# Cosine attention and a hard-swish feed-forward: shared items for the first pairs, transposing DMAs from item 8, a listed order of units, and a halved last unit

## The chip, the cores and the metric

The kernel runs on one core of one Trainium2 chip. The metric is the device time of one execution in microseconds (us). The median of three runs before the change is 427.83 us, the lowest 425.83 and the highest 430.05.

## The reference

```python
q_n = q / (norm(q) + 1e-6); k_n = k / (norm(k) + 1e-6)      # [8, 12, 448, 64], fp32
attn = softmax(q_n @ k_n.T / 0.1)                           # rows of 448
x = (attn @ v).transpose(0, 2, 1, 3).reshape(3584, 768)
h = x @ w_in                                                # 768 -> 2048
out = (h * clip(h + 3, 0, 6) / 6) @ w_out                   # 2048 -> 768, fp32
```

There are 8 batches of 12 heads, 448 rows a head and 64 columns a row. After the attention all heads of a row stand side by side and pass through two matrix products with a hard swish between them.

## The kernel before, in words

**Pairs and items.** The work on the attention goes by pairs of heads: pair i holds two heads of batch i // 6, so there are 48 pairs. The inputs come in by items: from item 2 on, item j holds q or k of two neighbouring pairs, 64 partitions for each of them and seven rows of a head in one partition (128 x 896 fp32, 448 KB). Items 2d and 2d+1 are q and k of pairs 2d and 2d+1; from `XJ` on the order is k first. Only items 0 and 1 are different: item 0 is pair 0 alone, q in the lower 64 partitions and k in the upper, and item 1 is pair 1 in the same way. They come by four DMAs each, half of them from ScalarE's queue.

**Steps.** The whole order of the first 18 pairs is written out by hand in `PLAN` (L19), a list of tokens that `run` (L659) takes one by one. Each engine gets its instructions in this order and waits, in order, for what they need. The tokens are:

- `LQ.j` loads item j (`load_qk`, L165), `LV.d` loads v of pairs 2d and 2d+1 (`load_v`, L186), both on SyncE's (SP's) queue. `W` starts the next of eight loads of the weights (L607), four of `w_in` and then four of `w_out`, from GpSimd (POOL), which cast to bf16.
- `SQ.j.e.c.n` squares n of the columns of item j from column c, on the engine e: v is VectorE (DVE), p is POOL, a is ScalarE (ACT). `RE.j` sums the squares (DVE), `NO.d` makes 1/norm of items 2d and 2d+1 from them with four small ACT instructions, and `NM.j.e` normalises item j into bf16.
- Then an item is transposed, in one of two ways. `TR.j` (L293) does it with seven matmuls into a PSUM bank, and `CQ.i` and `CK.i` copy q and k of pair i out of it. `XD.j` (`crossbar`, L304) does it with one transposing DMA on SP's queue, straight into a tile `tT` in SBUF; the scores read q from there, and only k is copied, by `CK.i` (L345). `CS.i` makes the last key block: by copies, or, after an XD, by two small POOL copies into `km` for two pairs at once. Even items of the second kind share one `tT` buffer, so the next even XD must wait for the `CK` and `CS` of the two pairs before it. Which way an item takes is set by `XJ`, which is 14 here (L105).
- `SC.i.g` are the scores of pair i in four groups, `EX.i.g` their exponentials on ACT, `VA.i.g` their products with v (PE). `VC.i` casts v to bf16 ahead of that. `FI.i` divides by the sums (DVE).
- The result is turned back into `xT`, again in one of two ways: `BK.i` with four matmuls and then `CX.i`, a copy from PSUM; or `XB.i` (`back_crossbar`, L492) with one transposing DMA on SP's queue.
- `U` issues the next unit of the feed-forward part on PE. There are two kinds: `mm1_unit` (L506), six matmuls of 448 columns that make one block of h for one batch (it needs `xT` of all six pairs of the batch; 16 per batch), and `mm2_unit` (L539), 16 matmuls of 384 columns that make a tile of the output (it needs all 16 blocks of h, and all weights loaded). `UA` and `UV` are what follows a unit: ACT's relu or copy, and DVE's product or copy with the store.
- `DP.n` and `D.n` are n matmuls on zeros, whose result nobody reads. `OPEN` changes over from PSUM tiles of two banks for the scores to a ring of six single banks.

**Which unit comes next** is set by `units` (L584), a rule for how many first and second products go with each pair; `stream` (L687) is the list made from it. The first 36 of them are issued by `PLAN`, and the rest by a loop over pairs 18 to 47 (L697), with three or four units a pair. After the last pair come the remaining units; the last `mm2_unit` has `end=True`: its output tile is copied in two halves of 64 partitions, the upper by ACT and the lower by DVE, and the second of its two stores goes from ACT's queue.

**SP's queue** runs in order as well: a DMA that waits for its input holds up all DMAs behind it. Eight semaphores are used in turn for it, so that at most eight DMAs are under way.

Of the kernel before, what the change touches and what calls it, by code (L numbers as in the profile page):

```python
# [60 lines left out]
def kernel(  # L61
# [43 lines left out]
    XJ = 14  # L105
# [59 lines left out]
    def load_qk(j, e="s"):  # L165
        needs(("NM", j - NR))
        raw_of[j] = raws[j % NR]
        if j < 2:
            for g in range(2):
                for i, x in enumerate((q, k)):  # L170
                    f = x[0, j + HP * g].rearrange("(p c) d -> p (c d)", c=7)
                    r = raw_of[j][64 * i : 64 * i + 64, g, :, :].rearrange("p c d -> p (c d)")
                    engines[e[i % len(e)]].dma_start(out=r, in_=f)
            return
# [6 lines left out]
    def load_v(d, e="s"):  # L186
        needs(("VC", 2 * (d - NV)), ("VC", 2 * (d - NV) + 1))
        b, n = 2 * d // HP, 2 * d % HP
        for g in range(2):
            f = v[b, HP * g + n : HP * g + n + 2].rearrange("i (p c) d -> p i (c d)", c=7)  # L190
            t = vr[d % NV][:, 2 * g : 2 * g + 2, :, :].rearrange("p i c d -> p i (c d)")
            for half in range(2):
                o = t[64 * half : 64 * half + 64, :, (1 - half) * D : (5 - half) * D]
                engines[e].dma_start(out=o, in_=f[:, :, 3 * half * D : (3 * half + 4) * D])
# [127 lines left out]
    def source(i, keys_of):  # L322
        j, x = (i, keys_of) if i < 2 else (i // 2 * 2 + (keys_of ^ (i >= XJ)), i % 2)
# [7 lines left out]
    def copy_q(i, e="v"):  # L331
        needs(("SM", i - 4))
        z, x, key = source(i, 0)
        if i >= 2:
            copy(e, qT[i % 4][:, 0:S], z[:, :, x, :])
            return
        q2 = qT[i % 4][:, 0:S].rearrange("p (c e) -> p c e", e=64)
        for h, n in ((0, 4), (1, 3)):
            o, f = q2[:, 4 * h : 4 * h + n, :], z[:, h : h + 2 * n - 1 : 2, x, :]
            if e == "a":  # L340
                nc.scalar.copy(out=o, in_=f)
            else:
                nc.vector.tensor_copy(out=o, in_=f)
# [195 lines left out]
    def mm2_unit(b, t, m, end=False):  # L539
        assert not weights  # L540
        g = gT[(b // 2) % 2]
        ps, key = bank_of(None, 1)
        for fc in range(FCN):
# [9 lines left out]
        cols = slice(m * MH, (m + 1) * MH)  # L553

        def store():
            o = sb.tile([128, MH], FP32, name="o", tag="o", bufs=4)
            if end:
                nc.scalar.copy(out=o[64:128, :], in_=ps[64:128, 0:MH])
                nc.vector.tensor_copy(out=o[0:64, :], in_=ps[0:64, 0:MH])
            elif on_act:  # L560
                nc.scalar.copy(out=o[:, :], in_=ps[:, 0:MH])  # L561
            else:
                nc.vector.tensor_copy(out=o[:, :], in_=ps[:, 0:MH])  # L563
            unread[key] = 0
            for e in range(2):
# [4 lines left out]
                eng = nc.scalar if end and e else nc.sync  # L570
                eng.dma_start(out=r[:, cols], in_=o[64 * e : 64 * e + 64, :])
# [208 lines left out]
```

## Time and profile before

| what | value |
|---|---|
| three runs, median | 427.83 us |
| the profiled execution, its own time | 426.68 us |
| its span, from the first to the last instruction | 424.7 us |
| PE, DVE, ACT, POOL busy in the span | 410.5, 220.1, 271.4, 184.0 us |
| DMA: moved, mean rate | 65.04 MB, 153 GB/s |
| XD (`tT<-nrm`): count, median from issue to landing | 34, 3.2 us |
| XB (`xT<-on`): count, median from issue to landing | 36, 3.5 us |
| loads of q and k, of v, of weights: median to landing | 4.3 to 4.6, 4.1, 9.0 to 9.6 us |
| clock granted to PE, mean | 0.997 |

The span is the part that the profile shows; 1.98 us of this execution's time lie outside of it. Busy time is an average over parts of the kernel with different limits, so the stretches of the span have to be read one by one. Matmuls are pipelined, and PE counts as busy in many of the short gaps between them: to see how well it is used, the work in a stretch has to be summed from the units.

### The profile page before, as it was taken

The numbers are of one execution on the slowest core, as the hardware profiler recorded it, in microseconds if no ns is written. First come the engines' busy times: TensorE is split into PE (matmuls) and PEld (weight loads), VectorE is DVE, ScalarE is ACT, GpSimd is POOL, SyncE is SP. The second block draws the span as 40 slices with busy tenths as digits, with TensorE's granted clock in tenths as the row PEclk, the third lists the DMA queues.
The fourth block names the chain that finished last, engine by engine and source line by source line (L and its number), as shares of the span: only waits on it lengthen the run. The fifth ranks groups of instructions, "written<-read, shape, count | busy, mean of one in ns | idle before, by whom it ended". The sixth has DMA issues, their size and how long they took to land.

```text
span 424.7 us, 9220 instructions
## 1 busy us (share of the span) xinstructions
PE 410.5 (97%) x3561; PEld 241.0 (57%) x3561; DVE 220.1 (52%) x427; ACT 271.4 (64%) x593; POOL 184.0 (43%) x188
## 2 busy tenths in 40 slices
PE   5899899999999999999999999999999999999995
PEld 2666456455655556555555555555555555655563
DVE  6896888856335554565455454555554343315411
ACT  4999799868547765766766775676765775105400
POOL 6997488515504555364464464374462200000000
PEclk9999999999999999999999999999999999999998
DMA  7999799998849769666978767667666241230033
GB/s 231 310 192 294 142 285 184 203 212 206 183 103 195 183 168 149 165 172 150 178 190 136 177 154 160 163 167 170 164 158 96 68 69 32 69 75 20 0 76 75
DMA packets 90828, 65.04 MB, mean 153 GB/s; under 512 B 55456, under 2 KB 89248, under 8 KB 90784
## 3 DMA queue, kind: packets, MB, share of 16 engines
q1 hardware_dynamic: 86672, 57.60, 59.1%
q0 software_dynamic: 3712, 6.29, 8.4%
q10 hardware_dynamic: 400, 0.56, 0.5%
q8 instruction: 28, 0.46, 0.5%
q14 instruction: 16, 0.13, 0.1%
HBM read 47.19 MB, written 11.01 MB: 137 GB/s over the span
## 4 chain that ended last, share of the span: by engine, by line
PE 80%; DMA 4%; DVE 2%; ACT 2%; POOL 1%; SPq 1%; issue 1%; POOLq 0%; DVEq 0%; ACTq 0%
PE M L546 22%; PE M L512 19%; PE PV L449 9%; PE Y L546 6%; PE Z L546 6%; PE Z L512 5%; PE M L410 5%; PE Y L512 5%; DMA tT<-nrm 3%; DMA vr<-in_v_dram 2%; PE Y L410 1%; PE Z L410 1%; DVE n L222 1%; ACT at L428 1%; DVE gT L527 1%
## 5 line engine op out<-in xcount | busy, mean ns | idle before, releaser
L546 PEld LDWEIGHTS <-gT 128*128 128x128 bf16 x896 | 87.4, 98 | 59.3 <-issue 0.2
L428 ACT ACTIVATE at<-M 128x448 bf16<-128x448 f32 x203 | 98.2, 564 | 28.0 <-PE M L410 17.9
L512 PEld LDWEIGHTS <-w_in_sb 128*128 128x128 bf16 x768 | 74.0, 98 | 66.8 <-issue 2.9
L512 PE MATMUL M<-xT,w_in_sb 128*128 128x448 bf16 x498 | 102.3, 353 | 0.2 <-DVE gT L527 0.2
L546 PE MATMUL M<-w_out_sb,gT 128*128 128x384 bf16 x576 | 97.9, 326 | 0.0
L253 POOL TENSOR_TENSOR nrm<-raw,r 128x896 bf16<-128x896 f32 (+1 forms) x48 | 79.7, 1666 | 37.6 <-ACT r L241 32.3
L527 DVE SCALAR_TENSOR_TENSOR gT<-u,M 128x448 bf16<-128x448 bf16 x83 | 51.3, 619 | 47.0 <-ACT u L521 45.5
L210 POOL TENSOR_TENSOR sq<-raw 128x896 f32<-128x896 f32 (+5 forms) x43 | 65.8, 1535 | 15.7 <-DVE n L222 8.4
L449 PEld LDWEIGHTS <-at 128*128 128x128 bf16 x1344 | 53.7, 98 | 24.0 <-issue 16.8
L521 ACT ACTIVATE u<-M,half_bias 128x448 bf16<-128x448 f32 x83 | 54.0, 651 | 19.9 <-PE M L512 18.2
L449 PE MATMUL PV<-vx,at 128*128 128x65 bf16 (+1 forms) x1344 | 64.4, 198 | 0.1
L222 DVE TENSOR_REDUCE n<-sq 128x14 f32<-128x896 f32 (+1 forms) x50 | 51.7, 1040 | 2.6 <-POOL sq L210 2.1
L367 POOL COPY km<-tT 64x128 bf16<-64x128 bf16 x34 | 9.8, 289 | 96.5 <-DMA tT<-nrm 34.4
L410 PE MATMUL M<-tT,kz 64*128 64x448 bf16 (+1 forms) x181 | 33.3, 353 | 2.2 <-DMA tT<-nrm 0.9
L428 ACT ACTIVATE at<-Z 128x448 bf16<-128x448 f32 x47 | 26.6, 566 | 11.8 <-PE M L410 11.8
L465 DVE TENSOR_TENSOR on<-PV,rc 128x512 bf16<-128x512 f32 x48 | 33.2, 691 | 1.9 <-DVE rc L464 0.2
L561 ACT COPY o<-M 128x384 f32<-128x384 f32 x19 | 9.1, 478 | 39.0 <-PE M L546 35.2
L546 PE MATMUL Y<-w_out_sb,gT 128*128 128x384 bf16 x176 | 30.4, 326 | 0.0
L563 DVE COPY o<-M 128x384 f32<-128x384 f32 x16 | 8.9, 558 | 41.3 <-PE M L546 41.3
L512 PE MATMUL Z<-xT,w_in_sb 128*128 128x448 bf16 x138 | 29.9, 353 | 0.0
L428 ACT ACTIVATE at<-Y 128x448 bf16<-128x448 f32 x44 | 25.1, 570 | 5.6 <-PE Z L410 5.3
L512 PE MATMUL Y<-xT,w_in_sb 128*128 128x448 bf16 x132 | 28.6, 353 | 0.0
(82 smaller groups left out, 333.5 us busy)
## 6 DMA issues: line engine op xcount, KB each, us to landing
vr<-in_v_dram SPq DMA_DIRECT2D x96, 128.0 KB, 4.1
out_dram<-o SPq DMA_DIRECT2D x111, 96.0 KB, 2.2
raw<-in_k_dram SPq DMA_DIRECT2D x23, 448.0 KB, 4.6
raw<-in_q_dram SPq DMA_DIRECT2D x23, 448.0 KB, 4.3
w_in_sb<-in_moe_w_in_dram POOLq DMA_DIRECT2D x4, 768.0 KB, 9.6
w_out_sb<-in_moe_w_out_dram POOLq DMA_DIRECT2D x4, 768.0 KB, 9.0
xT<-on SPq DMA_TRANSPOSE x36, 3.5
tT<-nrm SPq DMA_TRANSPOSE x34, 3.2
```

The lines of the kernel that those rows point to most:

```text
L210: engines[e].tensor_tensor(out=o, in0=i, in1=i, op=ALU.mult)
L222: nc.vector.tensor_reduce(out=n2s[d % 2][:, j % 2, c], in_=sq[:, :, :, :].rearrange("p g c d -> p (g c) d")[:, c, :], axis=AX.X, op=ALU.add,)
L253: engines[e].tensor_tensor(out=nrm[:, :, g, :].rearrange("p c g d -> p g c d"), in0=raw_of[j][:, g, :, :], in1=rs[d % 2][3][:, j % 2, :] . ...
L367: nc.gpsimd.tensor_copy(out=km[p, :, p], in_=z[p, 3, :, :])
L410: nc.tensor.matmul(o, ks, qt[rows], start=True, stop=True)
L428: nc.scalar.activation(out=o, in_=x, func=AF.Exp, scale=inv_tau)
L449: nc.tensor.matmul(o, at[:, n, q_cols(i // HP, j)], mv, start=(name == "A0" and j % 2 == 0), stop=last, skip_group_check=True,)
L465: nc.vector.tensor_tensor(out=on[:, :, :, :].rearrange("p (b j) h d -> p b (j h) d", b=2), in0=pv4[:, :, :, 0:D], in1=rc[:, :, :].to_broad ...
L512: nc.tensor.matmul(ps[:, 0:S], w_in_sb[:, cc, fc * 128 : (fc + 1) * 128], x[:, cc, 0:S], start=(cc == 0), stop=(cc == CC - 1),)
L521: nc.scalar.activation(out=u[:, :], in_=ps[:, 0:S], func=AF.Relu, bias=half_bias[:, :], scale=1.0 / 6.0)
L527: nc.vector.scalar_tensor_tensor(out=g[:, fc, c0 : c0 + S], in0=u[:, :], scalar=1.0, in1=ps[:, 0:S], op0=ALU.min, op1=ALU.mult,)
L546: nc.tensor.matmul(ps[:, 0:MH], lhs, w_out_sb[:, fc, m * MH : (m + 1) * MH], start=(fc == 0), stop=(fc == FCN - 1),)
```

## The change

Five things change.

1. Items 0 and 1 become like the others: item 0 is q of pairs 0 and 1, item 1 is k of them. `LQ.0` is one DMA, `LQ.1.1` and `LQ.1.0` are two, one for each head of the pairs, all on SP's queue. Their copies `CQ` and `CK` are then as for other items.
2. `XJ` goes from 14 to 8: items 8 to 13 are transposed by DMA instead of PE. In the list, pairs 6 to 11 are also turned back by `XB` instead of `BK` and `CX`.
3. The first 80 units are taken in the order of kinds that a string `ORDER` lists. Both orders issue 30 first and 6 second products in the list; in the new one all second products come after 29 first ones, in the old one the first comes after 23.
4. `PLAN` has another order throughout, with other engines for some squares, copies and casts. The last weight loads come later in it, and it has 82 matmuls of `DP` in 31 places instead of 55 in 12.
5. The last unit of all is split into two of 192 columns. Each half is copied by one engine and stored; the second store of the last half goes from ACT's queue.

```diff
-PLAN = [
-    "LQ.0.sa D.10 LQ.1.sa SQ.0.v.0.4 SQ.0.v.4.3 SQ.0.a.7.5 SQ.0.p.12.1 SQ.1.a.4.1 SQ.0.p.13.1 LQ.3 RE.0.0",
...
-    "SC.7.1 SC.7.2 TR.9 VA.6.3 EX.7.1 W EX.7.2 CS.8.a SQ.10.a.0.7 SC.7.3 CK.8.a U U VC.7.v CS.9.v U FI.6 CK.9.v",
-    "RE.11 EX.7.3 UA SQ.13.a.0.3 RE.10 UA UV BK.6 U VA.7.0 UA UA SQ.13.p.3.4 UV VA.7.1 SC.8.0 U NO.5 NM.10.p UV UA",
...
+ORDER = "11111111111111111111111111111222212211221112111211221112111121121111122111211121"
+PLAN = [
+    "LQ.0 LQ.1.1 SQ.0.v.6.2 SQ.0.a.0.6 LQ.1.0 LQ.3 SQ.1.a.7.4 SQ.0.v.8.6 SQ.1.a.11.3 DP.5 RE.0.0 RE.0.1 SQ.1.p.4.3",
+    "RE.1.1 SQ.1.a.0.4 DP.2 RE.1.0 NO.0.0 SQ.3.a.0.7 DP.3 NM.0.v.1 NM.0.v.0 NO.0.1 RE.3 LQ.2 NM.1.p.1 DP.2 D.10",
+    "TR.0.Y DP.7 LQ.5 SQ.2.a.0.7 NM.1.p.0 RE.2 DP.2 SQ.5.p.0.7 TR.1.Z DP.2 NO.1 LQ.6 LQ.4 CK.0.v NM.2.p DP.2",
+    "CQ.0.v DP.3 CK.1.v SC.0.0.0 DP.2 DP.3 LV.0 SC.0.1.1 DP.5 SQ.4.a.0.7 NM.3.p LV.2 CQ.1.v EX.0.0 SC.0.2.0 EX.0.1",
...
+    "CX.5.v VC.7.v VC.9.p VA.6.2 EX.7.2 U VA.6.3 RE.12 CK.8.v EX.7.3 U UA SQ.13.a.0.7 SC.8.0 SQ.14.v.0.7 NO.5 U U",
+    "UA UV EX.8.0 U UA W FI.6 VA.7.0 W UV SC.8.1 UA UV UV SC.8.2 UA UV EX.8.1 CS.8.v VA.7.1 VC.8.v U SC.8.3",
+    "NM.10.p EX.8.2 VA.7.2 CK.9.v UA U RE.13 EX.8.3 NO.6 UA VA.7.3 UV NM.11.p SC.9.0 FI.7 EX.9.0 UV SC.9.1 U XD.10",
+    "VA.8.0 XD.11 SC.9.2 UA EX.9.1 VA.8.1 VA.8.2 RE.14 VA.8.3 EX.9.2 SQ.15.p.0.7 CK.10.v UV SC.9.3 EX.9.3 LV.6 U",
+    "SC.10.0 U NM.12.p UA SC.10.1 FI.8 EX.10.0 UV UA RE.15 SC.10.2 VA.9.0 EX.10.1 EX.10.2 CS.10.v UV W CK.11.v",
+    "LV.5 XB.6 U VA.9.1 VA.9.2 VC.10.p UA SC.10.3 U EX.10.3 UV XB.7 NO.7 VC.12.v VA.9.3 SC.11.0 SC.11.1 U UA",
+    "EX.11.0 NM.13.p XD.12 UA FI.9 XB.8 VA.10.0 XD.13 LQ.16 VA.10.1 UV CK.12.v VA.10.2 UV SC.11.2 EX.11.1 EX.11.2",
+    "VA.10.3 U VC.11.p SC.11.3 SC.12.0 NM.15.p SC.12.1 LV.7 FI.10 UA CS.12.v XB.10 EX.11.3 VA.11.0 VA.11.1 VA.11.2",
+    "NM.14.p EX.12.0 XB.9 UV SC.12.2 VA.11.3 FI.11 XB.11 SC.12.3 LQ.17 EX.12.1 U EX.12.2 EX.12.3 U VC.14.p VA.12.0",
+    "W CK.13.v UA SC.13.0 SC.13.1 SQ.16.p.0.7 UA EX.13.0 VA.12.1 UV VA.12.2 XD.14 EX.13.1 UV VA.12.3 SC.13.2 FI.12",
+    "W SC.13.3 EX.13.2 U U VC.13.a CS.14.v UA UA RE.16 EX.13.3 U UV U UA CK.14.v UV UV XD.15 VA.13.0 SQ.17.a.0.7",
...
-    XJ = 14
+    XJ = 8
...
-    def load_qk(j, e="s"):
+    def load_qk(j, *heads):
...
-        if j < 2:
-            for g in range(2):
-                for i, x in enumerate((q, k)):
-                    f = x[0, j + HP * g].rearrange("(p c) d -> p (c d)", c=7)
-                    r = raw_of[j][64 * i : 64 * i + 64, g, :, :].rearrange("p c d -> p (c d)")
-                    engines[e[i % len(e)]].dma_start(out=r, in_=f)
-            return
...
+        g = slice(heads[0], heads[0] + 1) if heads else slice(0, 2)
+        nc.sync.dma_start(out=raw_of[j][:, g, :, :].rearrange("p g c d -> p g (c d)"), in_=f[:, g, :])
...
     def source(i, keys_of):
-        j, x = (i, keys_of) if i < 2 else (i // 2 * 2 + (keys_of ^ (i >= XJ)), i % 2)
+        j, x = i // 2 * 2 + (keys_of ^ (i >= XJ)), i % 2
...
-    def mm2_unit(b, t, m, end=False):
+    def mm2_unit(b, t, m, end=None):
...
+        width = MH if end is None else MH // 2
+        cols = slice(m * MH + width * (end or 0), m * MH + width * (end or 0) + width)
...
-            if end:
-                nc.scalar.copy(out=o[64:128, :], in_=ps[64:128, 0:MH])
-                nc.vector.tensor_copy(out=o[0:64, :], in_=ps[0:64, 0:MH])
-            elif on_act:
-                nc.scalar.copy(out=o[:, :], in_=ps[:, 0:MH])
+            if on_act:
+                nc.scalar.copy(out=o[:, 0:width], in_=ps[:, 0:width])
...
-                eng = nc.scalar if end and e else nc.sync
+                eng = nc.scalar if end == 1 and e else nc.sync
...
     def second(b):
-        last = (B - 1, nt - 1, 1)
-        return [(mm2_unit, b, t, m, (b, t, m) == last) for t in range(nt) for m in range(2)]
+        u = [(mm2_unit, b, t, m) for t in range(nt) for m in range(2)]
+        return u if b < B - 1 else u[:-1] + [u[-1] + (0,), u[-1] + (1,)]
...
+    by_kind = {"1": [u for u in stream if u[0] is mm1_unit], "2": [u for u in stream if u[0] is mm2_unit]}
+    first = [by_kind[x].pop(0) for x in ORDER]
+    stream = first + [u for u in stream if u not in first]
```

## The prediction

> **What bounds the kernel now.** I read the page first (PE busy for 410.5 of 424.7 us), then busy time by stretch, cut at the first exponential (11.2), the end of pair 7's (43.9), the first of pair 8 (50), pair 13 (77), the end of the hand-written list (118.5) and the last matmul (420.8).
>
> ```profile
> 0.00:11.20 11.20, 6.73 (x37) 3.26 (x38) 6.56 (x32) 5.34 (x14) 7.59 (x24) 1.00 0.77 230
> 11.20:43.90 32.70, 30.12 (x401) 20.32 (x398) 25.62 (x57) 30.97 (x61) 27.33 (x22) 1.00 1.07 264
> 43.90:50.00 6.10, 4.84 (x50) 2.72 (x49) 5.79 (x10) 4.10 (x10) 1.66 (x2) 1.00 0.92 174
> 50.00:77.00 27.00, 27.00 (x298) 15.98 (x297) 21.98 (x47) 26.32 (x63) 23.09 (x20) 1.00 0.96 200
> 77.00:118.50 41.50, 40.41 (x328) 22.59 (x326) 23.99 (x44) 28.42 (x62) 17.84 (x17) 1.00 0.93 200
> 118.50:420.80 302.30, 301.44 (x2461) 176.10 (x2458) 135.65 (x239) 176.23 (x386) 106.53 (x105) 1.00 0.59 129
> 420.80:424.70 3.90, 0.00 (x0) 0.00 (x0) 0.55 (x1) 0.01 (x1) 0.00 (x0) 0.70 0.21 50
> ```
>
> The columns are PE, PEld, DVE, ACT, POOL, clock, DMA share, GB/s. Up to 77 us ACT is the limit (30.97 of 32.70, 26.32 of 27.00), with a hole at 43.9 to 50, and the DMA engines are full too (1.07, 0.92, 0.96). After 118.5 PE sets the time and all else has slack. The part in between hangs on transposing DMAs. The waits of the hole, one wait of PE, and the chain that ended last say so:
>
> ```profile
> ACT sq L208 <- DVE n L222: 1.7, 1, 1.7
> ...
> PE M L410 <- DMA tT<-nrm: 0.9, 1, 0.9
> ```
>
> ```profile
> 70.97 6.24 DMA tT<-nrm
> 77.23 0.35 DVE kz L357
> ...
> 95.20 4.47 DMA tT<-nrm
> ...
> 146.18 2.27 PE M L512 x12
> ...
> 149.59 2.60 PE Z L546 x16
> ```
>
> A transposing DMA holds up pair 14 (its SC.14.0 runs at 79.84, seen in the timeline) and pair 16. The median landing of this group is 3.2 us (page, part 6), but 6.24 here, with two weight loads under way (issued at 63.5 and 65.5, 9.0 to land). SP issues in order, and each issue costs it time (timeline of SP):
>
> ```profile
> 95.20 1.25 SPq L309 DMA_TRANSPOSE tT<-nrm  x1
> 96.50 0.57 SPq L179 DMA_DIRECT2D raw<-in_k_dram  x1
> 97.12 1.23 SPq L496 DMA_TRANSPOSE xT<-on  x1
> ...
> 100.20 6.12 SPq L194 DMA_DIRECT2D vr<-in_v_dram  x8
> ```
>
> So an XD or XB costs SP 1.3 us with the gap, an LQ 0.65, an LV (four DMAs) 2.6.
>
> **What does not change.** Both lists hold 36 units, 30 first and 6 second products, and the loop after them has the same units per pair. So the 302.3 us from 118.5 on stay, and only three pieces move: the list up to pair 14, from there to its end, and the tail. The new order and ORDER act inside the list; beyond it they only permute units whose price is fixed (2.27 us for two first products, 2.60 for a second, last two lines of the chain above).
>
> **Step 1, front to pair 7.** Pair 0 now needs items 0 and 1. q (448 KB, one DMA) and k's halves all leave SP by 2.6 us. In the old run DVE's first square of item 0 starts at 3.79 and ACT's, which waits for the last piece, at 5.19; I take 4.5 for 448 KB. Then by old rows: squares to 4.9, two reduces of 0.62 to 6.2, norms 1.05 to 7.4; k's reduces to 7.5; ACT squares item 3 (0.94) and does the second norms to 9.6; POOL normalises k in two halves of 0.94 to 11.5; transposes 0.55, copies 0.38 twice: SC.0.0 at 13.0 against 10.44. Before EX.0.0 ACT also gets SQ.3, NO.1 and SQ.4 (2.9 us), which used to come later or went elsewhere, so EX.0.0 starts at 13.7, 2.5 later, with more behind it. Summed over the tokens up to EX.7.3, ACT has 37.6 us of work against 37.8. I put EX.7.3's end at 43.1 instead of 43.9; bounds -1 to +2.3 on that gain, for if the 2.5 us were not recovered it is a loss of 1.5 to 2.3.
>
> **Step 2, the hole.** ACT's slice of SQ.13 waits 1.69 us for a reduce that waits for SQ.10 on ACT itself. Now SQ.10 to SQ.12 are POOL's and ahead of need, so the wait goes. ACT then does a relu, SQ.13, NO.5 and a relu (0.63, 0.95, 1.06, 0.63): EX.8.0 at 46.4 instead of 50.0. (Fewer relus lie before it; at equal work the gain is some 2.4.) What is late next is step 3.
>
> **Step 3, pairs 8 to 14: the transposes move to SP's queue.** Gone are six items' transposes on PE (7 in 0.39 us) and six on-chip back-transposes (0.22), 3.7 us of PE that lay beside ACT's work and so bring nothing by themselves; and some 8 us of DVE copies (0.38 and 0.62), also covered. In their place come six XD and six XB. An even XD waits for the copies of the pair before (one tT buffer), so XD.10 cannot leave before CK.9. DVE reaches that after EX.8.0's three following relus (49.2), a product 0.62, a cast 0.68 and the copy 0.35: 50.9. XD.11 leaves at 52.2. From there SP's order is fixed: XD.11, LV.6, LV.5, XB.6, XB.7, XD.12, XB.8, XD.13, LQ.16, LV.7, XB.10, XB.9, XB.11, LQ.17, XD.14, XD.15. That is ten transposes before XD.15 at 1.3, three LV at 2.6, two LQ at 0.65: 22.1 us. XD.15 leaves at 74.3, and SC.14.0 waits for it. Landing: 3.2 (median) or 6.2 (beside weights; W6 and W7 are issued near 70), so 77.5 to 80.5. I take 4.7, being between a clear and a crowded queue: SC.14.0 at 79.0 against 79.84. Steps 1 and 2 are thus mostly eaten by SP's queue. XB.11 leaves at 71.1 and lands by 74.6 (3.5, page); U16 needs it, and four units of 1.14 on PE lead from there to SC.14.0 too: 79.1, the same time. While XD.10 waits, LV.6 and LV.5 stand behind it on SP, and while XD.14 does, LQ.19; they are loads ahead of need (NM, SQ or casts some two pairs on), so nobody waits for them. Behind the waiting SC.14.0 on PE are U20 and on, behind its exponentials on ACT the relus, so a late XD stops all.
>
> [...]
>
> In the trace's DMA records a 256-byte packet takes 25.6 ns, an XD is 896 and an XB 512 of them: 1.43 and 0.82 us of all 16 engines. Six of each are 13.5 us more.
>
> [...]
>
> **Step 4, pair 14 to the list's end.** Before: 79.84 to 118.5, 38.7 us, for 11 first and 6 second products (12.5 + 15.6), four pairs' scores (0.76 each) and values (about 0.75): 34.5 of work, 4.1 of waits. After: one first product fewer, 33.2. In the steady part (130 to 330 us) the same sum fills 95.3% of the time, so 1.6 us of waits are the least, 4.1 the most if all stays; XD.16 and XD.17 are now far ahead of SC.16.0, so I take 3.0. The list ends at 79.0 + 33.2 + 3.0 = 115.2, 3.3 earlier. The 2.9 us of added DP dummies lie in PE's slack before pair 7; without that cover they would cost just these 2.9.
>
> **Step 5, the tail.** ACT's half copy and DVE's follow one another (timeline):
>
> ```profile
> 420.33 0.47 ACT L558 COPY o<-M 64x384 f32<-64x384 f32 x1 [2.08 <-PE M L546]
> ...
> 420.84 0.55 DVE L559 COPY o<-M 64x384 f32<-64x384 f32 x1 [5.15 <-ACT o L558]
> ```
>
> One copy of half the columns (0.3 to 0.35 by these rows) replaces 1.06; the first half's store lies under the second's 1.3 us of matmuls. Gain 0.7 (0 to 0.8).
>
> **Sum.** 3.3 + 0.7 = 4.0: span 420.7. The profiled run took 426.68, 1.98 outside the span: 422.7; the median of the runs is 1.15 above it: 423.9.
>
> **Rivals.**
> *A, slower: the DMA engines become the bound before pair 14.* For: the shares above give 66.5 us of DMA in 65.8. Plus 13.5, less the last weight load moved behind (8.4% of the span over 8 loads, 4.46): 75.5. At 1.07, the best stretch, that ends at 81.8; at 1.0 at 86.7. Against: 43.9 to 77 had some idle DMA time, and loads run ahead of need. It decides once SC.14.0 comes after 83.0 (118.5 + 0.7 - 33.2 - 3.0). At 86.7, with 4.1 of waits late: list end 124.0, 5.5 later, less 0.7: 432.6.
> *B: the shared items cost.* The 2.5 us at EX.0.0 stay, and SP's chain shifts by them: 426.4. For: pair 0 waits for twice the data. Against: ACT has 2.9 us of moved work to do there.
> *C: clean.* XD.15 lands in 3.2 and the late stretch runs like the steady part: 77.5 + 33.2 + 1.6 = 112.3, with the tail 6.9 gained: 421.0. Against: landings beside weight loads were 6.24.
>
> **Chances.** Forecast 0.38, A 0.30, B 0.10, C 0.22. About 1% (4.3 us) is what can be told from no change: faster is below 423.55, slower above 432.1. Faster: C, and a third of the forecast, 0.35. Slower: two thirds of A and a little for unseen waits, 0.21. The rest is 0.44. The forecast's own range is 421.5 to 427; the full range, C less the runs' 2 us to A, is 419 to 433.
>
> **What would show it.** ACT above 90% from EX.0.0 (13.7) to 43; EX.8.0 near 46.4; XD.15 leaving near 74.3 with SP busy before it; SC.14.0 near 79; SC.18.0 near 115; last matmul to end 3.2. Wrong if XD landings exceed 6 us or DMA share is above 1.07 throughout (A), if EX.7.3 ends after 45 (B), or if the loop behind the list differs from 302 us.

## The result and the profile after

The changed kernel takes 447.0 us (median of four runs, 446.45 to 454.06), the kernel before 428.9 us beside it: a ratio of 1.042, 95% interval 1.033 to 1.051. The run of 454.06, 1.7% above the fastest, counts as slow, and the ratio leaves it out. The change makes the kernel slower by 4%, where the prediction had 423.9 us and 433 as the end of its full range. The profiled execution took 446.63 us, its span is 444.6 (before: 424.7).

The times of the first score matmuls of single pairs, read from the trace, say where the 20 us arise:

| event | predicted | before | after |
|---|---|---|---|
| EX.0.0 starts | 13.7 | 11.2 | 13.1 |
| EX.7.3 ends | 43.1 | 43.9 | 47.3 |
| EX.8.0 starts | 46.4 | 50.0 | 50.0 |
| SC.11.0 | – | 63.9 | 66.1 |
| SC.12.0 | – | 69.3 | 76.2 |
| SC.14.0 | 79.0 | 79.8 | 96.4 |
| SC.18.0 (the list is done) | 115.2 | 118.5 | 134.3 |
| SC.47.0, behind the kernel before | | | +20.5 |

First busy time by stretch in the changed kernel (columns as in the prediction: PE, PEld, DVE, ACT, POOL, clock, DMA share, GB/s), cut at the same events as before:

```profile
13.06:47.26 34.20, 29.09 (x382) 18.36 (x381) 26.08 (x51) 28.50 (x54) 27.49 (x23) 1.00 1.05 246
50.01:77.00 26.99, 23.01 (x219) 12.34 (x218) 15.86 (x30) 20.77 (x49) 12.79 (x13) 0.94 0.91 162
77.00:134.25 57.25, 47.43 (x402) 26.70 (x399) 30.11 (x50) 35.55 (x80) 20.42 (x20) 0.94 0.92 175
...
134.25:440.80 306.55, 302.85 (x2477) 177.40 (x2474) 135.12 (x239) 176.09 (x385) 110.50 (x108) 1.00 0.57 130
```

From 50 to 77 us ACT was busy for 26.3 of 27.0 us before; now it is for 20.8, and no other engine is full either. The third row is 57 us long where it was 41.5. The engines wait, and the waits of the changed kernel from 60 to 105 us (engine and line, what it waits for: us, times, longest) name what for:

```profile
POOL vx L265 <- DMA vr<-in_v_dram: 12.3, 2, 9.7
...
DVE kz L341 <- DMA tT<-nrm: 9.3, 1, 9.3
...
PE M L394 <- DMA tT<-nrm: 7.8, 1, 7.8
...
DVE on L449 <- DMA xT<-on: 4.7, 1, 4.7
```

They are landings of transposing DMAs and of a load of v. The chain that ended last runs through the same transfers (start, duration):

```profile
62.85 8.16 DMA xT<-on
...
80.61 3.88 DMA xT<-on
...
86.21 10.12 DMA tT<-nrm
...
108.56 5.79 DMA raw<-in_k_dram
```

In the code's names: XB.6 lands late, and since `on` has three buffers, the division FI.9 waits for it; then U16 waits for XB.11, SC.14.0 for XD.15, and DVE's squares of item 18 for LQ.18. What was issued beside XD.15, which takes 10 us to land, is seen in the timelines of SP's and of POOL's queue:

```profile
77.98 3.83 SPq L480 DMA_TRANSPOSE xT<-on  x3
81.85 1.46 SPq L174 DMA_DIRECT2D raw<-in_q_dram  x1
83.43 8.36 SPq L302 DMA_TRANSPOSE tT<-nrm  x2
...
81.79 0.81 POOL L591 DMA_DIRECT2D w_out_sb<-in_moe_w_out_dram  x1
84.25 0.81 POOL L591 DMA_DIRECT2D w_out_sb<-in_moe_w_out_dram  x1
```

XD.14 is issued at 83.4, between two weight loads, and XD.15 at 86.2, behind both. The issue of the two, 2.6 us in e13 below, holds SP for 8.4 (XD.15 alone 5.6), and they land 12.1 and 10.1 us after its start.

### The profile page after: what moved, and what is told of

The parts are those of the page before. It is cut to its first block, busy times and chain, and to the rows that moved or that the text cites. A ratio compares the mean times of both kernels' runs of the same rounds, so it can differ in the third digit from the quotient of the medians.

```text
span 444.6 us, 9168 instructions
## 1 busy us (share of the span) xinstructions
PE 414.5 (93%) x3538; PEld 241.7 (54%) x3538; DVE 219.0 (49%) x407; ACT 272.0 (61%) x592; POOL 178.8 (40%) x185
## 4 chain that ended last, share of the span: by engine, by line
PE 74%; DMA 8%; ACT 6%; issue 3%; DVE 3%; SPq 3%; POOL 3%; POOLq 0%; ACTq 0%; DVEq 0%
PE M L532 20%; PE M L496 17%; PE PV L433 8%; PE Y L532 6%; PE Z L532 6%; DMA xT<-on 5%; PE M L394 4%; PE Y L496 4%; PE Z L496 4%; ACT at L412 3%; DMA tT<-nrm 2%; SPq L186 2%; POOL nrm L246 1%; PE PV L603 1%; PE Z L394 1%
## 5 line engine op out<-in xcount | busy, mean ns | idle before, releaser
L532 PEld LDWEIGHTS <-gT 128*128 128x128 bf16 x912 | 88.7, 98 | 59.6 <-issue 1.3
L496 PE MATMUL M<-xT,w_in_sb 128*128 128x448 bf16 x546 | 112.7, 355 | 0.1
L532 PE MATMUL M<-w_out_sb,gT 128*128 128x384 bf16 (+1 forms) x592 | 98.1, 322 | 1.2 <-DVE gT L511 1.2
L246 POOL TENSOR_TENSOR nrm<-raw,r 128x896 bf16<-128x896 f32 (+1 forms) x44 | 73.5, 1674 | 30.4 <-ACT r L234 25.5
L203 POOL TENSOR_TENSOR sq<-raw 128x896 f32<-128x896 f32 (+1 forms) x39 | 64.5, 1653 | 30.4 <-DMA raw<-in_q_dram 13.5
L394 PE MATMUL M<-tT,kz 64*128 64x448 bf16 x165 | 32.4, 356 | 8.7 <-DMA tT<-nrm 7.8
L449 DVE TENSOR_TENSOR on<-PV,rc 128x512 bf16<-128x512 f32 x48 | 33.2, 692 | 6.3 <-DMA xT<-on 4.7
L545 DVE COPY o<-M 128x384 f32<-128x384 f32 (+1 forms) x20 | 11.0, 548 | 51.0 <-PE M L532 51.0
L543 ACT COPY o<-M 128x384 f32<-128x384 f32 (+1 forms) x17 | 8.0, 469 | 40.8 <-PE M L532 38.9
L448 DVE RECIPROCAL rc<-PV 128x8 f32<-128x8 f32 x48 | 9.9, 206 | 38.4 <-PE PV L433 33.9
L265 POOL CAST vx<-vr 128x512 bf16<-128x512 f32 x37 | 23.5, 637 | 12.4 <-DMA vr<-in_v_dram 12.3
L532 PE MATMUL Z<-w_out_sb,gT 128*128 128x384 bf16 x160 | 27.6, 326 | 0.0
```

The lines of the kernel that those rows point to most:

```text
L203: engines[e].tensor_tensor(out=o, in0=i, in1=i, op=ALU.mult)
L246: engines[e].tensor_tensor(out=nrm[:, :, g, :].rearrange("p c g d -> p g c d"), in0=raw_of[j][:, g, :, :], in1=rs[d % 2][3][:, j % 2, :] . ...
L265: (engines[e].copy if e == "a" else engines[e].tensor_copy)(out=o, in_=f)
L394: nc.tensor.matmul(o, ks, qt[rows], start=True, stop=True)
L449: nc.vector.tensor_tensor(out=on[:, :, :, :].rearrange("p (b j) h d -> p b (j h) d", b=2), in0=pv4[:, :, :, 0:D], in1=rc[:, :, :].to_broad ...
L496: nc.tensor.matmul(ps[:, 0:S], w_in_sb[:, cc, fc * 128 : (fc + 1) * 128], x[:, cc, 0:S], start=(cc == 0), stop=(cc == CC - 1),)
```

## The experiments

All ratios are to the kernel before on the same chip. "Pair 14 +8" means that SC.14.0 comes 8 us behind its 79.84 in the kernel before, in the profiled run. My theory after this reading: transposing DMAs (and loads) that run beside casting weight loads land late, and PE, ACT or DVE wait for the next one. Rivals: the transposing DMAs cost by themselves (their sum, or SP's order); the new order of the list costs; the front's dummies cost. There is one trace of each kernel, and its early marks scatter: with the kernel before's own front (e11, e12, e15, e16, e17), SC.8.0 comes from 1.3 us ahead of the kernel before to 1.6 behind it.

### e1: PE transposes put back into the changed kernel

```diff
-    XJ = 8
+    XJ = 14
-  XD.8 ... XD.13        XB.6 ... XB.11
+  TR.8 ... TR.13 with CQ, CK, CS       BK.6 CX.6 ... BK.11 CX.11
```
Four unit finishers, EX.11.1, SC.12.3 and BK.11 had to move by a few tokens, as the kernel asserts that a PSUM bank has been read before it is taken again (`bank_of`).

> The changed kernel with items 8 to 13 transposed by PE again and pairs 6 to 11 turned back by PE again (XJ = 14, BK and CX in place of XB); its front, order of units, weight loads and halved last unit stay. Theory (late transposing DMAs): PE's waits for tT and xT between 60 and 101 us cost some 18 us, and the PE transposes give 5 back, so 447 falls to 430 to 434, and SC.14.0 comes near 83 instead of 96.4. Rival (the new order itself, its dummies and units, is what costs): 440 or more, with SC.14.0 after 90.

Measured 441.4, 1.033 (1.029 to 1.036). Pair 14 is at +11.9 instead of +16.5, that is at 91.8. These are the rival's numbers (440 or more, and after 90), and the theory's were missed. What the waits name is something else again: with the copies on DVE again, in places that I chose, the transposes of PE come late, and POOL waits 8.7 us to normalise ("nrm L247 <- PE M L292"). So the run shows that transposing DMAs need not be the whole of it, and doesn't tell what the new order costs with PE transposes in better places.

### e2 and e13: weight loads left out

```diff
     def next_weights():
         o, w = weights.pop(0)
-        nc.gpsimd.dma_start(out=o, in_=w)
+        if len(weights) >= 3:                     # e2; e13: >= 4 or not weights
+            nc.gpsimd.dma_start(out=o, in_=w)
-                w_out_sb[:, fc, cols],
+                w_out_sb[:, fc % 4, cols],        # e13: 12 + fc % 4
```

> The changed kernel without the last three weight loads (4.7 MB of 12.6 as fp32): the second products use the first quarter of w_out four times, so PE's work is the same. Theory (transposing DMAs land late because other transfers fill the DMA engines): the landings of tT between 80 and 100 us fall from 11 to 3 to 5, SC.14.0 moves from 96.4 to 85 or earlier, total 433 to 438. Rival (SP's queue in order and the three on buffers): SC.14.0 stays after 92, total 443 or more.

> The changed kernel without the first three loads of w_out: only the last, issued at 100 us, is made, and the second products use that quarter of w_out four times; PE's work is the same. From 55 to 100 us no weight load runs. Theory (weight loads beside them make the transposing DMAs and the loads of v late): SC.12.0 stands 1 to 3 us behind the kernel before instead of 6.9, SC.14.0 3 to 5 behind instead of 16.5, total 429 to 433. Rival (the transposing DMAs and loads are late by their own sum and SP's order): SC.12.0 stays 5 or more behind, total 435 or more.

e2: 436.5, 1.023 (1.018 to 1.028); pair 12 +6.5, pair 14 +8.9. e13: 433.4, 1.017 (1.012 to 1.021); pair 12 +3.2, pair 14 +5.7, e2's total is in its range, its pair 14 is later than hoped (88.7 for 85), and e13 is slightly above on all three. Same kernel, same transposes, same order of SP: without three of the eight weight loads 10 us (1.042 to 1.017) are gone. e2 keeps the fifth weight load (issued at 61.0), and pair 12 is nearly as late as in the changed kernel; in e13 that load goes, and pair 12 gains 3.7 us. The DMA issues (count, median us from issue to landing), first of the changed kernel and then of e13, each from 50 to 76 and from 76 to 100 us:

```profile
w_out_sb<-in_moe_w_out_dram POOLq DMA_DIRECT2D x1, 768.0 KB, 8.5
...
xT<-on SPq DMA_TRANSPOSE x3, 7.1
...
w_out_sb<-in_moe_w_out_dram POOLq DMA_DIRECT2D x2, 768.0 KB, 9.4
...
tT<-nrm SPq DMA_TRANSPOSE x2, 11.1
```
```profile
xT<-on SPq DMA_TRANSPOSE x4, 2.9
...
tT<-nrm SPq DMA_TRANSPOSE x4, 3.9
```

7.1 becomes 2.9 and 11.1 becomes 3.9. That is the theory's size.

### e3 and e5: the transposing DMAs alone in the kernel before

```diff
 e3:  XJ = 8, TR.8..13 -> XD.8..13 without CQ and the odd CS; BK.6..11, CX.6..11 -> XB.6..11
 e5:  as e3, and
-  W CX.4.v EX.6.2 ... EX.7.1 W EX.7.2 SQ.10 SC.7.3 CS.8 CK.8 ... CK.9
+  CX.4.v EX.6.2 ... EX.7.1 EX.7.2 SQ.10 SC.7.3 CS.8 W CK.8 ... CK.9 W
```

> The kernel before with that part alone: items 8 to 13 by XD (XJ = 8), pairs 6 to 11 by XB, in the old order of the list and with the old front, units and last unit. Theory (the added transposing DMAs are late beside loads and weights): SC.14.0 goes from 79.8 to 88 or later, total 435 to 442. Rival (they are harmless, and the loss comes of the new order): 426 to 430.

> The kernel of e3 with two weight loads moved: the third and fourth stand behind the POOL copies CS.8, which wait for XD.8, instead of ahead of XD.8 and XD.9. Nothing else changes. Theory (a transposing DMA beside a casting weight load lands late, and PE waits for it): the landing of XD.9, 16.7 in e3, falls to 6 or less, SC.8.0 moves from 11.3 us behind the kernel before to 2 to 4 behind, and the total from 456.8 to 446 to 451 (the loss at pairs 13 and 14 stays). Rival (SP's order and the loads of v in front of it, whatever the weights do): XD.9 still takes over 10, total 454 or more.

e3: 456.8, 1.068 (1.062 to 1.073), worse than the whole change and above the expected range; pair 14 is at +31.0. e5: 456.4, 1.068 (1.061 to 1.074), no better, though its first half came true: pair 8 goes from +11.3 to +1.1. The chain of e3 has XD.9, and SP's timeline of e5 has XD.9 and a later XD:

```profile
41.46 16.70 DMA tT<-nrm
```
```profile
43.60 1.25 SPq L308 DMA_TRANSPOSE tT<-nrm  x1
...
84.05 12.79 SPq L308 DMA_TRANSPOSE tT<-nrm  x1
```

In e3 XD.9 is issued 4.2 us behind the third weight load and 0.7 ahead of the fourth, and takes 16.7 us. In e5 the loads start 0.9 and 1.6 us behind it; its issue takes 1.25 us, and it lands in 3.1: ahead of the weight loads it is not late. XB.6, issued 2.1 us after it and so behind both loads, takes 11.8. Later XD.14, XB.9 and XD.15 (78.6 to 84.1) stand beside the next weight loads (74.4, 81.8 and 86.3). XD.15, the second line, takes 21.4 us to land, and pair 14 is at +31.7 against +31.0. What was gained at pair 8 is lost again. So a local cause shows in a local mark, and need not show in the total.

### e4: without the late dummies

```diff
-  every DP behind FI.0 in the list
```

> The changed kernel without the DP dummies that stand behind FI.0 in the list (25 of 82 and more). Rival on the front (the dummies write the PV bank, so that the division waits for them and they for it): EX.7.3 ends 3 to 4 us sooner than 46.4, and as the late transposes do not wait for the front the total falls by 0 to 4, to 443 to 447. Theory (the front's loss is swallowed by the DMA queue behind it): total within 1 us of 447. If the granted clock falls without them, EX.7.3 ends later.

Measured 445.3, 1.042 (1.040 to 1.045), the ratio of the changed kernel itself. EX.7.3 ends at 43.6 instead of 47.3, and EX.8.0 starts at 46.3 instead of 50.0. The rival named this (3 to 4 us sooner). The dummies cost 3.7 us of the front in this pair of traces: they write the bank of PV, so that the waits of the changed kernel from 14 to 47 us read

```profile
DVE rc L448 <- PE PV L603: 4.4, 3, 2.5
...
PE PV L603 <- DVE on L449: 2.7, 2, 1.9
```

DVE waits for dummies, and dummies for DVE. Over more traces the price is some 3 us: EX.7.3 ends at 47.2 to 48.4 in seven runs with these dummies (the changed kernel, e2, e6 to e9, e13), and at 43.6 to 45.7 in the four without (e4, e10, e14, e18). By pair 14 (+14.9) more than half of e4's gain is swallowed.

### e6, e14, e15, e16: weight loads moved

```diff
 e6 (changed kernel):   W.6 and W.7 from VA.12.0 and FI.12 to behind VC.15.p
 e14 (e10, see below):  W.5 to W.7 behind VC.15.p, ORDER = "1" * 32 + "2222"
 e15 (kernel before):   W.6 to W.8 behind CS.14, ORDER = "1" * 29 + "2222122", halved last unit
 e16: e15 with XB.6 to XB.11 in place of BK and CX
```
(In e14 to e16 a few UA and UV moved with the kinds of units.)

> The changed kernel with its sixth and seventh weight loads moved behind CS.14 and VC.15 on POOL, so that they start after XD.14 has landed instead of just before it leaves. Theory: XD.14 and XD.15 land in 3 to 5 us instead of 10 to 12, SC.14.0 comes near 88 instead of 96.4; the first second product may then wait some 2 us for the weights; total 439 to 443. Rival (any transfer in the queue does the same): SC.14.0 after 93, total 445 or more.

> The kernel of e10 with the first load of w_out moved as well, so that all four are issued behind VC.15 on POOL (from 87 us on), and with 32 first products ahead of the first second one in the list instead of 29, since the last load then lands near 106. Theory: pair 12's 6.5 us behind the kernel before goes to 1 to 3, and the total from 431.7 to 426 to 429, level with the kernel before. Rival (the loads put off come back as a wait of the second products, or of the loads beside them): 431 or more.

> The kernel before with its last three weight loads moved behind CS.14 on POOL, which waits for XD.14, 29 first products ahead of the first second one, and the halved last unit. In the kernel before XD.14 or XD.15 took 6.24 us to land beside two weight loads, and PE waited. Theory: it lands in 3 to 4, SC.14.0 comes 1 to 3 us sooner than 79.84; if the weights are in time for the 30th unit the total falls by 1 to 3, to 424 to 426, below both kernels. Rival (the weights come too late, or beside XD.16): 427 to 431.

> The kernel of e15 with XB for pairs 6 to 11. In e12 the same XB cost 14 us, nearly all at pair 14, where the 17th unit waited 10.6 us for XB.11 beside weight loads. Theory (the weight loads beside it made it late): XB.11 lands in 3 to 5 us, SC.14.0 stands 0 to 4 behind the kernel before instead of 15.2, total 426 to 431. Rival (XB is late by SP's order): SC.14.0 10 or more behind, total 436 or more.

e6 came as expected, half a us below its range: 438.5, 1.026 (1.019 to 1.034), pair 14 +8.1, that is at 87.9; XD.14 and XD.15 land in 4.0 and 2.9 us. The other three missed: e14 and e16 have the rival's totals, and e15 lies above both ranges. e14: 441.3, 1.034 (1.031 to 1.038): pair 12 +1.3 and pair 14 +3.4 as wanted, but now XD.16 and XD.17 stand beside four weight loads (83.8 to 87.7), DVE waits 9.8 us for `tT`, and pair 17 is at +14.2. e15: 437.8, 1.025 (1.021 to 1.028): pair 14 +1.5, not earlier, and from there a load of k is beside three weight loads (chain):

```profile
87.77 8.99 DMA raw<-in_k_dram
```

Pair 17 is at +10.7. e16: 449.5, 1.054 (1.050 to 1.058), pair 14 +18.1; this one missed its aim, as POOL reached its three weight loads at 74.7 and XB.11 was issued at 77.2, right behind them. The kernel before, with its last four loads in two pairs (63.5 and 65.5, 74.2 and 75.5), is better than every place that I tried for them.

### e7 and e8: the order behind the list, and the buffers of on

```diff
 e7: -ORDER = "1111...2211112..."   (80 kinds)      +ORDER = its first 36
 e8: -tag="on", bufs=3 ... needs(..., ("BK", i - 3))
     +tag="on", bufs=4 ... needs(..., ("BK", i - 4))      rc: bufs=1
```

> The changed kernel with the listed order cut to its first 36 units, those that the list issues; from pair 18 on the units come by the old rule. The prediction took the loop behind the list as unchanged (302.3 us), yet it lost 4.7 us between pairs 18 and 27. Theory (the listed order of units 37 to 80 does that, and nothing else): pair 47's first scores stand as far behind the kernel before as pair 18's (15.8), total 442 to 443. Rival (the loss is the late pairs' DMAs, whatever the units): 446 to 447.

> The changed kernel with four on buffers instead of three (rc has one instead of two, for space). Theory (the late landing of XB.6 is passed on to PE by the division that waits for its buffer): SC.12.0 moves from 6.9 us behind the kernel before to 2 to 4 behind; the wait for XD.15 behind it swallows most of that, total 444 to 447. Rival (the buffers are the main limit of the whole stretch): 441 or less. If neither, SC.12.0 stays.

e7: 446.3, 1.045 (1.040 to 1.050). From pair 18 to 47 it loses 1.1 us where the changed kernel loses 4.7, but its list came 3.7 later in the profiled run, and the total is the rival's. e8: 446.6, 1.047 (1.040 to 1.053); its total is in the theory's range, but pair 12 is at +5.6 instead of +6.9, which is neither. With the buffer there, the chain shows the next late transfer, XD.12, in the same place:

```profile
66.12 6.86 DMA tT<-nrm
```

### e9 and e10: repairs on top of e6

```diff
 e9:  -  XD.10 VA.8.0 XD.11 ... LV.6 ... LV.5 XB.6 ... XB.7
      +  LV.5 XD.10 VA.8.0 XD.11 ... XB.6 ... XB.7 LV.6
 e10: e9, LQ.18 behind LQ.19, no DP behind FI.0, ORDER cut to 36
```

> The kernel of e6 with two loads of v moved on SP's queue: LV.5 goes ahead of XD.10 instead of behind XD.11, and LV.6 behind XB.7 instead of ahead of XB.6 and XB.7. The prediction said that nobody waits for them. Theory (the eight DMAs take SP 5.3 us, XB.6 leaves that much later, the division of pair 9 waits for its buffer, and the cast of pair 10 waits 9 us for LV.5): XB.6 leaves near 57.6 instead of 62.9, SC.12.0 moves from 6.2 us behind the kernel before to 1 to 3 behind, total 3 to 5 below e6, 434 to 436. Rival (the DMA engines are full there, whatever the order): within 1 of e6's 438.5.

> The kernel of e9 with three more edits: LQ.18 directly behind LQ.19 (ahead of XD.17 on SP), no DP behind FI.0, and the listed order cut to 36 units. If each wait found in the trace of the changed kernel counts by itself, 447 loses 8.5 (weights), 4 (loads of v), 3 (LQ.18), 1.5 (DP) and 1 (order of the loop): 428 to 431, within 1% of the kernel before. Rival (what one wait gives back the next takes, as with the buffers in e8): 434 or more.

e9: 437.8, 1.026 (1.023 to 1.029): no gain, the rival's total. XB.6 leaves at 57.3 as expected, but LV.6 then stands beside the fifth weight load (issued at 60.2), and the cast behind it on DVE waits:

```profile
61.84 8.31 DMA vr<-in_v_dram
```

Pair 12 is at +7.0. e10: 431.7, 1.011 (1.007 to 1.015), just above the range expected. The ratio went from 1.042 to 1.026 by the weights' place in e6, and from there to 1.011 by the smaller repairs together: about half each.

### e11: the halved last unit alone

```diff
-        return [(mm2_unit, b, t, m, (b, t, m) == last) ...]
+        return u if b < B - 1 else u[:-1] + [u[-1] + (0,), u[-1] + (1,)]
```

> The kernel before with the halved last unit alone. Theory: the end behind the last matmul gets 0.7 us shorter (0 to 0.8), total 0.7 below the kernel before, which the runs can just not tell. Rival (the second set of 16 weight loads and a store more on SP eat it): 0 to +0.5. In the changed kernel the last matmul to the end was 3.8 us instead of 4.4.

Measured 426.41 against 426.69, 0.999 (0.997 to 1.001). In the trace the end of the last matmul to the end of the span is 3.7 us against 4.4: the 0.7 is there, and the runs can't tell it.

### e12 and e17: XB alone in the kernel before

```diff
 e12: BK.6 .. BK.11 with CX.6 .. CX.11  ->  XB.6 .. XB.11
 e17: e12 with the weight loads as in e2
```

> The kernel before with XB for pairs 6 to 11 alone; items 8 to 13 stay with PE. Theory (SP's six additional issues come late beside the weight loads, but xT is read only from the 17th unit on, so only the buffers of on can be missed): 2 to 8 us slower than before, 429 to 435, far less than e3's 29. Rival (XB is as costly as XD): 440 or more. If faster than before, the move of the back-transposes was the good part of the change.

> The kernel of e12 (before, with XB for pairs 6 to 11) without the last three loads of w_out; the second products use the first quarter of w_out four times, PE's work is the same. Theory (XB.11's 10.6 us are due to the weight loads beside it): it lands in 3 to 5, SC.14.0 stands 0 to 3 us behind the kernel before instead of 15.2, total 425 to 431. Rival (XB is late by SP's order): SC.14.0 10 or more behind, total 437 or more.

e12: 440.6, 1.032 (1.029 to 1.034), pair 14 +15.2: the rival's numbers, and my "far less" was wrong. e17: 432.2, 1.010 (1.008 to 1.013), pair 14 +6.9, between the two. The DMA issues from 76 to 100 us, e12 and then e17:

```profile
xT<-on SPq DMA_TRANSPOSE x2, 10.5
```
```profile
xT<-on SPq DMA_TRANSPOSE x3, 4.0
```

So beside weight loads XB (10.5 us here) is no better than XD (11.1 in the changed kernel), and without them some 1% of loss stays: XB.11 leaves at 78.7, and the 17th unit waits 3.1 us for it, where PE in the kernel before, with BK and CX, shows no wait from 72 to 78 us.

### e18: everything at once

```diff
 e13, with e10's other edits: LV.5, LV.6 and LQ.18 moved, no DP behind FI.0, ORDER cut to 36
```

> The kernel of e13 (no weight load between 55 and 89 us) with the other four repairs of e10: LV.5 and LV.6 moved, LQ.18 behind LQ.19, no DP behind FI.0, the listed order cut to 36 units. Theory (weight loads beside the transposing DMAs, the front's dummies, LQ.18 and the order of the loop are the whole loss): pair 47 stands 0 to 3 us behind the kernel before instead of 20.5, total 425 to 429. Rival (the added transposing DMAs cost by themselves as well): 431 or more.

Measured 427.9, 1.001 (0.998 to 1.005): level with the kernel before, pair 47 at +1.7, with all twelve added transposing DMAs in it. Since three weight loads are left out, this is no version to use (the kernel before without them was not run); it says that these causes together are as large as the loss. How much of that is the kernel's own gain from moving less data, which the kernel before would have too, stays open, and so does a small cost of the added transposes by themselves. None of the versions that do the whole work is measurably faster than the kernel before.

## Why the prediction was wrong

Step 3 failed, and with it the sign. It priced the landing of XD.15 at 4.7 us, where it took 10.1, and put the waits for LV.5 and for XB.6's buffer at nothing, so that XD.15 left at 86.2 and not at 74.3. Steps 1 and "What does not change" failed by some 4 us each.

**Step 1, front.** SC.0.0 and EX.0.0 came at 12.5 and 13.1 (13.0 and 13.7 predicted). EX.7.3 ended at 47.3 instead of 43.1. The failed term is the sentence that 2.9 us of added dummies lie in PE's slack: they share a bank with the division, and cost some 3 us. Without them it is 43.6 in e4, half a us from the forecast, but up to 45.7 in e10, e14 and e18, so that e4's closeness is partly luck. The old front's own traces end EX.7.3 at 43.9 to 46.3 (the kernel before, e11, e12, e15 to e17). So rival B was right in the sign of its loss at EX.7.3, but the dummies were its cause, and no cost of the shared items is left to see there.

**Step 2, the hole.** ACT's wait for the reduce is gone, and from the end of EX.7.3 to EX.8.0 it takes 2.7 us instead of 6.1. EX.8.0 comes at 50.0 all the same because of step 1, and at 46.3 in e4 (46.4 predicted; 47.2 to 48.4 in e10, e14 and e18).

**Step 3, the error of sign.** XD.15 was to leave at 74.3 and land in 4.7. It left at 86.2 and took 10.1: 11.9 and 5.4 us late, together the 17.4 at SC.14.0. Of the first, some 4 were there when XB.6 left (62.9; the sum's own chain gives 58.7), most of it from the front. (With the front in time, in e4, XB.6 still left at 62.6: DVE had to wait for the load of item 14, and the issues took longer.) Some 2 more came from the issues of XD.12 and XB.8, 2.8 and 2.0 us for the 1.3 of the sum. Then "nobody waits" for LV.6 and LV.5 proved wrong: POOL waited 9.7 us for LV.5, NM.13 stood behind that, and XD.13 could leave only when NM.13 was done, at 73.0, 9 us later than in the sum's chain. All that stands behind it on SP, XB.11 too, was late by this. XB.6 took 8.2 to land, and I had let nobody wait for it either; but FI.9 does, for its buffer, and PE stood for 4.0 us. The last 2 us or so came from the issues of LQ.17 and XD.14 beside weight loads (1.5 and 2.7).

The deeper fault was to price a landing by something near its median (4.7) although the chain shown had a late one, 6.24 us beside weight loads (two more were issued during it, at 74.2 and 75.5), and the change puts twelve more transposes into a stretch with six of the eight weight loads (32.6 to 84.3 us). e13, which leaves out three of them, puts some 10 us on that.

**Rival A** had the right direction and the wrong mechanism. It let the DMA engines' sum set the end and came to 86.7 for SC.14.0; its mark, a share above 1.07 throughout, did not appear (0.91 and 0.92 from 50 to 134 us). But while XB.6 and XD.15 were under way the engines were full. The same two stretches in the changed kernel and, below, in e13 (the DMA share is the last number but one):

```profile
62.00:71.00 9.00, 5.88 (x56) 2.97 (x55) 3.06 (x6) 7.24 (x18) 0.31 (x1) 1.00 1.25 171
82.00:97.00 15.00, 6.37 (x43) 3.09 (x40) 4.09 (x8) 6.33 (x13) 4.22 (x6) 0.85 1.13 203
```
```profile
62.00:71.00 9.00, 9.00 (x98) 5.06 (x97) 6.09 (x13) 8.82 (x22) 3.83 (x4) 1.00 0.68 138
82.00:97.00 15.00, 14.89 (x105) 7.59 (x102) 9.81 (x17) 12.47 (x26) 6.96 (x7) 1.00 0.71 152
```

So it was not the sum over the whole stretch that set the end, but single transfers, late one after the other where the engines were full for some us. Whether a transposing DMA lands late there because of that, or because of something that only a casting load brings, isn't shown: no run has a plain load of the same size in its place. Beside other loads two were somewhat late as well: XB.13 and XD.16 of the changed kernel, issued at 109.2 and 110.5 between loads of k and v and behind the last weight load's landing, took 5.6 and 5.2, where the medians of their groups are 3.7 and 2.8. But full engines for a short time were not always enough: in e13 the share was 1.14 and 1.10 in the two stretches of 2 us from 82 to 86, and XD.15, issued at 81.8, landed in 3.6.

**Step 4.** SC.14.0 to SC.18.0 took 37.9 us for 36.2 predicted. One part of the extra is LQ.18, issued behind XD.17, as DVE has to wait for it to square item 18: where LQ.18 was moved (e10, e18) the piece takes 35.4, in the runs of the changed list where it wasn't, 36.2 to 38.9. (e14 moved it too, but has four weight loads here, and took 48.4.) PE's clock (below) may be another; it was not tested. (The parts of the sum add to 34.1 us of work, not 34.5, and to 33.0 with one product fewer, not 33.2.)

**"What does not change": 302.3 us.** It was 306.6. The listed order of units 37 to 80 is a change in that stretch, and I had called it a mere permutation. The chain runs through two XBs there (at 144.1, 4.8 us, and at 190.1, 3.5 us). With the order cut, 1.1 (e7), 2.5 (e10), 2.7 (e14) and 1.8 (e18) are lost there instead of 4.7; with it, between 1.8 and 4.7 in the other runs. What the order itself costs stays open.

**Step 5.** The gap behind the last matmul is 3.8 us, 4.4 before: 0.6 gained for 0.7 predicted. (The table of before was cut half a us late, hence the 3.2.)

## What to carry to other kernels

Price a DMA that an engine will wait for by the worst landing that the trace shows in such company, not by the median of its group, and list for each one what is in flight beside it; here casting loads of 768 KB just ahead of it turned medians of 3 to 4 us (e13) into 7 to 11 (the changed kernel), and single landings into up to 21 (e5). Follow every buffer that such a DMA reads from or writes to, since the division that reuses a buffer waits as surely as the reader (FI.9 for XB.6, 4.7 us). Where several late transfers stand in a row, mending one may move no total (e4, e5, e8, e9): judge a repair by the mark of its own place, and the whole by taking all the causes away at once.

## What the runs showed of the hardware

The issue of a transposing DMA on SP isn't a fixed price. It took 1.25 us in the median of the 34 XD of the kernel before (1.23 to 2.6), but 5.6 (XD.15 in the changed kernel), 9.4 (XD.9 in e3) and 12.8 us (XD.15 in e5) beside weight loads, and everything behind it in SP's queue waited: no DMA behind it left before 91.8, 52.0 and 96.9.

Two long waits of PE cost clock as well. While PE waits for XD.15 the granted clock (the column before the DMA share) falls, and it comes back only some 3 us after the work has:

```profile
92.00:94.00 2.00, 0.00 (x0) 0.00 (x0) 0.00 (x0) 0.91 (x2) 0.00 (x0) 0.64 1.15 202
...
96.00:98.00 2.00, 1.63 (x7) 0.48 (x8) 2.00 (x4) 0.98 (x2) 0.87 (x2) 0.50 0.46 160
98.00:100.00 2.00, 2.00 (x9) 0.87 (x8) 0.72 (x2) 0.38 (x1) 1.40 (x1) 0.65 0.00 0
```

PE is idle from 88.5 to 96.4, where SC.14.0 starts. In finer stretches of the same trace the clock is 1.00 up to 92.5, 0.50 from 92.6 to 99.2 and 1.00 again from 99.4: it falls some 4 us after the work stopped. The wait for FI.9 shows the same: PE is idle from 67.9 to 71.9, and the clock is 1.00 up to 72.0, 0.50 from 72.2 to 75.4 and 1.00 from 75.6, so that it falls again some 4 us after the work stopped and comes back some 3.6 us after it went on. A shorter wait, 2.5 us for the XB issued at 144.1, leaves the clock at 1.00. The 4 us are no fixed figure: in the kernel before the last matmul ends at 420.3, and the clock is 0.50 from 422.4 on.
